# Another order of the loads and of the early attention work, and the last lane of the last projection in two token halves

## The chip, the cores and the metric

The kernel runs on one core of a Trainium2 chip. The metric is the device time of one execution in microseconds (us); the number given for a kernel is the median of its runs.

## The reference

Sparse attention feeds a network without nonlinearities. Attention has 4 batches, 8 heads, 768 tokens and a head size of 64; every query sees the keys less than 16 positions away, and one summary per block of 32 keys (the maximum of the keys, the mean of the values). The network follows on 3072 tokens of 512 numbers, in fp32:

```python
scores_l = scale * q @ k.T                 # kept where |i - j| < 16
scores_s = scale * q @ k_sum.T + log(32)   # k_sum: max over each block of 32 keys
a = softmax(concat(scores_l, scores_s))
x = a @ concat(v, v_sum)                   # v_sum: mean over each block
h = (x @ w1) * (x @ w2)                    # 512 -> 1024
out = (h @ w3) @ w_out                     # 1024 -> 1024 -> 512
```

## The kernel before

**The work.** Tokens are taken in six units u of 512, heads in four pairs, so attention has 24 steps called pairs here: pair 4u+p. A pair is: scores of q and k on TensorE (`sc`, line 374), a fused masked minimum on VectorE (line 388), exponentials on ScalarE (line 402), reciprocals of the sums (lines 407 and 408), the normalization, transposes on TensorE (`tp`, line 432), their copies to SBUF (`pt`, lines 437 to 441), the product with the values (`po`, line 452), and the attention output `x` kept as a rounded high part (line 478, ScalarE) and the rest (line 121, VectorE). Line 121 is the helper `low`, which makes every such rest.

All large products are made of three: high by high, low by high, high by low. Weights come from HBM as 64-bit numbers in 1 MB pieces (`wraw`, line 156), 20 of them: four of w_out and eight of w3 first, then w1 and w2 by turns. Each piece is converted: ScalarE takes the upper word (line 176); the low bits are joined to it either by VectorE alone (lines 203 and 206) or by ScalarE (line 188) and one VectorE instruction (line 194); then ScalarE rounds the high part (line 220) and VectorE makes the low part (line 121). The order's names number the converted pieces: in the rows of before, `w_323` is the last half of the first four w3 tiles, `w_395` the last piece of w_out (the eighth piece of all), `w_434` the first whole tile of w3 (the ninth). TensorE first multiplies w3 by w_out (`mm<-w,w`, folded weights `wp`, stored by line 247 and line 121), while the first four pairs of attention are put between; these are followed by the classic gates and projection of the first 1024 tokens (`mm<-x,w`, `mm<-wp,h`). The other 2048 tokens, in two groups of 1024, go through a Strassen-like scheme of 7 products instead of 8 (`ln`, line 727): gates `ln<-xT,ws`, and a projection `ln<-hT,ws`, whose products are evacuated and added up at lines 745 (ScalarE) and 747 (VectorE) and sent to HBM at line 894.

**The last projection.** `project_fast` calls `lanes` with two lanes (the two 128-row halves of a 256-row block of the transposed output), one PSUM bank each. It runs over seven products k = 0 to 6, in the groups (0, 1), (2, 3), (4, 5, 6) that accumulate in the bank; in each product lane 0 and then lane 1 makes 12 matmuls (4 steps of 3 terms), a 128x128 stationary by 512 tokens, and after each lane's 12 VectorE (or, for the first sums, ScalarE) adds the bank to the sum in SBUF. Products 1, 4, 5 and 6 complete a quarter of the output, and line 894 sends it.

**What sets the order.** The program of TensorE and of the DMA queue (SP) is written in numbered slots t. The table `LOADS` says which load follows the issue of which weight piece, `WORK` what is put into which slot, `FIRST` the slots in which pairs 0, 1, 2, 3 and the four after them begin. Strings choose the engine: `LAST_BITS` (a letter per weight piece) who joins the low bits, `NORMALIZE` (a letter per pair 0 to 7) who normalizes: A is eight ScalarE instructions (line 418), P one GpSimd instruction (line 421), V one on VectorE. `SECOND` says who copies the second transposed half; `first_pair` reads it for pairs 0 to 3 and `four_pairs` for pairs 4 and 5, and from pair 6 on the copies are made in `lump`, which doesn't read it. The order on ScalarE and VectorE in this part is a scheduler's. SP works its DMAs off in order, and a DMA whose buffer is still in use holds up all behind it: `q` has two buffers, so the q of one pair waits for the scores two fetches earlier; the fetches are in the order 0, 1, 2, 3, 5, 4, so q of pair 4 waits for the scores of pair 3.

Of the kernel before, what the change touches and what calls it, by code (L numbers as in the profile page):

```python
# [11 lines left out]
F32 = mybir.dt.float32  # L12
# [4 lines left out]
ALU = mybir.AluOpType  # L17
# [3 lines left out]
P = 128  # L21
# [23 lines left out]

LAST_BITS = "VVVVVVVVAAAAVVVVVVVV"
NORMALIZE = "APAPPVVV"
SECOND = "VAAVVAVV"  # L50

BANKS = "SSTTTTST"
SOONER = 400
# [20 lines left out]
def attention_moe(ctx, tc, qG, kW, kT, vP, vW, vB, mask, w1, w2, w3T, wo, out, outT):  # L74
    nc = tc.nc
    B, NPAIR, _, S = kT.shape
    S -= PAD
    NB = S // BLOCK
    U = TOKENS
# [269 lines left out]
    def keep_means(b):  # L349

        nc.sync.dma_start(vS[b], vs[b])
# [203 lines left out]
    NSU = NU // 2  # L555
# [156 lines left out]
            flow.pop(0)[1](t)  # L712
            ready.append(t)

    def lanes(n, o, weights_of, moving_of, steps, evacuated, tags, between=None):

        banks = [ps.tile([P, 512], F32, name="ln", tag=tag, bufs=bufs) for tag, bufs in tags]
        for at, k in enumerate(o.ids):
            stationary_of = yield from weights_of(at, k)
            for i in range(n):  # L720
                for c in range(steps):
                    if between and c % KH == 0:
                        between(at, i * steps // KH + c // KH)
                    a, m = [stationary_of(i, c, w) for w in range(2)], moving_of(k, c)
                    terms = [(a[0], m[0]), (a[1], m[0]), (a[0], m[1])]
                    for j, (x, y) in enumerate(terms):
                        nc.tensor.matmul(  # L727
                            banks[i][:, :U],
                            lhsT=x,
                            rhs=y,  # L730
                            start=c + j == 0 and k in o.first,
                            stop=c == steps - 1 and j == 2 and k in o.last,
                            skip_group_check=True,
                        )
                    if c < steps - 1:
                        yield 3 * U
                with tc.high_priority(offset=SOONER):
                    evacuated(at, k, i, banks[i][:, :U])
                yield 3 * U

    def add_up(o, k, parts, got):

        to, more = o.adds[k]
        if more is None:
            nc.scalar.copy(parts[to], got)
        else:
            nc.vector.tensor_tensor(parts[to], got, parts[more], ALU.add)  # L747

    xT, raws, kept, hT, tasks, background = {}, {}, {}, {}, [], []

# [23 lines left out]
    def gates(n, whole):  # L774


        o = ORDERS[n]
        for r in range(NF // 4):
            if r == NF // 4 - 1:
                flow.extend(output_flow(k, c) for k in LATE.ids for c in range(2))  # L780
                if n + 1 < NSU:
                    gates_flow(n + 1)

            def weights_of(at, k):
                while (n, k) not in xT:
# [12 lines left out]
            def evacuated(at, k, i, got):  # L798
                if at == 0:
                    parts.append(whole.parts(i))  # L800
                add_up(o, k, parts[i], got)
# [65 lines left out]
    def project_fast(n, whole):  # L867
        parts = []

        def between(at, j):  # L870
            with tc.high_priority(offset=SOONER // 2):
                if j < 3 and at + 2 < NK:
                    for work in whole.moving(at + 2):
                        next(work, 0)
            if n + 1 < NSU and j == 3 and at in (4, 5):
                moving_x(n + 1, at - 4)

        def weights_of(at, k):
# [7 lines left out]
        def evacuated(at, k, i, got):  # L886
            if at == 0:
                parts.append((*temporary(), *temporary()))
            add_up(LATE, k, parts[i], got)
            done = {1: (0, 0, 2), 4: (0, 1, 3), 5: (1, 1, 1), 6: (1, 0, 0)}  # L890
            if k in done:
                half, u, t = done[k]
                rows, cols = half * DH + i * P, (n - 1) * 2 * U + u * U
                nc.sync.dma_start(outT[rows : rows + P, cols : cols + U], parts[i][t])

        tags = [("mm", 2), ("mm", 2)]
        yield from lanes(2, LATE, weights_of, lambda k, c: hT[n, k][c], NF // 2, evacuated, tags, between)

    def spill_weights(q):

# [109 lines left out]
    def fill(s):  # L1010
        if s < NS:
            gather(*place(s), inputs[s][1])
# [103 lines left out]
    LOADS = {  # L1116
        4: [lambda: keys(0)],
        7: [lambda: nc.sync.dma_start(mask_sb, mask)],
        9: [lambda: fetch(0), lambda: rows(0, 1)],
        12: [lambda: fetch(1)],  # L1120
        13: [lambda: rows(0, 0)],
        15: [lambda: rows(0, 2)],
        16: [lambda: keys(2), lambda: fetch(2)],
        17: [lambda: keys(1)],
        19: [lambda: keys(3)],
        20: [lambda: fetch_values(0)],
        22: [lambda: fetch(3)],
        23: [lambda: fetch_values(1), lambda: fetch_values(2)],
        26: [lambda: fetch_values(3)],
    }  # L1130
    WORK = {
        11: [lambda: first_keys(0), lambda: fill(0)],
        13: [lambda: means(0)],
        14: [lambda: first_keys(1)],
        17: [lambda: fetch_sums(0)],
        18: [lambda: fill(1), lambda: load_second(0)],
        19: [lambda: rows(1, 2)],
        20: [lambda: rows(1, 0), lambda: first_keys(2), lambda: fill(2)],
        21: [lambda: rows(1, 1), lambda: fetch(5), lambda: fetch_sums(2)],
        22: [lambda: first_keys(3), lambda: fetch(4), lambda: fill(3), lambda: fetch_sums(1), lambda: load_second(1)],  # L1140
        25: [lambda: second_batch(0), lambda: load_second(2), lambda: fetch(6)],
        29: [lambda: load_second(3)],
        30: [lambda: means(1), lambda: fetch_sums(3)],
        31: [lambda: second_batch(1), lambda: fetch_values(4)],
        32: [lambda: fetch_values(5), lambda: second_batch(3)],
        33: [lambda: second_batch(2), lambda: fetch_sums(4)],
        35: [lambda: keep_means(1)],
        38: [lambda: fetch_sums(5), lambda: fill(4), lambda: fill(5)],
        40: [lambda: fetch(7), lambda: fill(6)],
        47: [lambda: fill(7)],  # L1150
# [208 lines left out]
```

## Time and profile before

| | |
|---|---|
| median of three runs | 514.44 us |
| the three runs | 510.35, 514.44, 514.94 us |
| the profiled execution | 510.71 us |
| its span, first to last instruction | 508.9 us |
| TensorE (PE) busy | 487.1 us, 96% of the span |
| VectorE (DVE) busy | 356.8 us, 70% |
| ScalarE (ACT) busy | 318.4 us, 63% |
| GpSimd (POOL) busy | 43.5 us, 9% |
| mean granted TensorE clock | 0.998 |

PEld is TensorE's weight load, which has rows of its own. In a timeline a row gives start, duration, engine, line, operation, what it writes and reads, the number of instructions that are merged, and in brackets how long the engine was idle before it and who released it. Neighbouring matmuls overlap in the records. A few rows' durations overlap the next row's start by about 0.1 us, so the step from one start to the next is the better measure in a busy stretch.

### The profile page before, as it was taken

The page shows a single profiled execution, that of the slowest core. Times are in us where ns is not written, and L with a number is a line of the kernel's source. Part 1 is how long each engine was busy: PE and PEld are TensorE (multiplying, and loading weights), DVE is VectorE, ACT ScalarE, POOL GpSimd, SP SyncE. Part 2 cuts the span into 40 slices and gives each one's busy share as a digit, 9 for nine tenths or more (in the row PEclk, how much of TensorE's full clock was granted, in tenths as well). Part 3 has the DMA queues.
Part 4 walks back from the last instruction along what each step waited for, and adds up shares of the span by engine and source line. Part 5 has one row for each costly group of instructions (what it writes and reads, how often), then busy time and mean ns, then how long its engine had stood idle before and what let it go on. Part 6 is the DMA issues. An engine that isn't in the chain of part 4 may idle for free.

```text
span 508.9 us, 10455 instructions
## 1 busy us (share of the span) xinstructions
PE 487.1 (96%) x3792; PEld 390.2 (77%) x3792; DVE 356.8 (70%) x870; ACT 318.4 (63%) x882; POOL 43.5 (9%) x86
## 2 busy tenths in 40 slices
PE   0889998999999999999999999999999999999996
PEld 0667776888887777777777877877788888888885
DVE  4978866898814598984558895899977029129972
ACT  5589975567726788877897587657865421513710
POOL 1022323101210210000000000000000000000000
PEclk9999999999999999999999999999999999999999
DMA  8998749999589989879998899998778655555762
GB/s 341 406 412 274 288 151 363 316 374 406 186 257 314 284 288 280 252 264 341 311 318 269 296 308 300 350 340 259 220 253 253 225 194 184 201 184 189 216 199 83
DMA packets 57460, 139.29 MB, mean 274 GB/s; under 512 B 6208, under 2 KB 19008, under 8 KB 54848
## 3 DMA queue, kind: packets, MB, share of 16 engines
q1 hardware_dynamic: 55104, 134.43, 77.5%
q0 software_dynamic: 1152, 2.10, 2.6%
q10 hardware_dynamic: 1152, 2.10, 1.1%
q8 instruction: 30, 0.49, 0.4%
q14 instruction: 22, 0.18, 0.1%
HBM read 105.89 MB, written 32.70 MB: 272 GB/s over the span
## 4 chain that ended last, share of the span: by engine, by line
PE 85%; DMA 5%; DVE 5%; ACT 4%; issue 1%; SPq 0%
PE ln L727 46%; PE mm L125 28%; PE po L452 4%; PE sc L374 4%; DMA wraw<-in_wo_dram 3%; PE tp L432 2%; DMA wraw<-in_w_dram 2%; DVE wf L206 2%; DVE w L121 1%; ACT w L220 1%; ACT sm L402 1%; ACT wf L176 1%; DVE wf L203 1%; ACT sm L418 0%; ACT wp L247 0%
## 5 line engine op out<-in xcount | busy, mean ns | idle before, releaser
L727 PE MATMUL ln<-xT,ws 128*128 128x512 f32 x672 | 157.0, 392 | 0.0
L727 PEld LDWEIGHTS ln<-xT,ws 128*128 128x128 f32 x672 | 125.0, 188 | 27.6 <-issue 0.6
L125 PE MATMUL mm<-x,w 128*128 128x512 f32 x384 | 91.1, 394 | 0.7 <-ACT x L478 0.5
L125 PEld LDWEIGHTS mm<-x,w 128*128 128x128 f32 x384 | 71.0, 188 | 17.4 <-ACT x L478 0.9
L402 ACT ACTIVATE sm<-sm,mx 128x120 f32<-128x120 f32 x192 | 74.0, 390 | 7.8 <-DVE mx L388 7.6
L727 PE MATMUL ln<-hT,ws 128*128 128x512 f32 x336 | 78.3, 392 | 0.0
L747 DVE TENSOR_TENSOR tmp<-ln,tmp 128x512 f32<-128x512 f32 x52 | 35.8, 688 | 55.4 <-PE ln L727 41.2
L727 PEld LDWEIGHTS ln<-hT,ws 128*128 128x128 f32 x336 | 62.6, 188 | 13.4 <-DVE hT L121 0.2
L125 PE MATMUL mm<-w,w 128*128 128x512 f32 x192 | 50.5, 411 | 15.5 <-ACT w L220 12.7
L638 ACT CAST hT<-hr 128x512 fp32r<-128x512 f32 x56 | 32.1, 622 | 42.5 <-DVE hr L804 35.4
L125 PEld LDWEIGHTS mm<-w,w 128*128 128x128 f32 x192 | 36.0, 194 | 26.8 <-ACT w L220 13.8
L388 DVE CUSTOM_DVE_ANT_0 sm<-sc,mask_sb 128x120 f32<-128x120 f32 x192 | 42.3, 276 | 15.1 <-PE sc L374 15.0
L125 PE MATMUL mm<-wp,h 128*128 128x512 f32 x192 | 46.3, 395 | 0.0
L412 ACT ACTIVATE sm<-sm,mx 128x120 f32<-128x120 f32 x128 | 38.8, 386 | 6.1 <-DVE mx L408 6.1
L125 PEld LDWEIGHTS mm<-wp,h 128*128 128x128 f32 x192 | 35.4, 188 | 8.0 <-issue 0.5
L121 DVE TENSOR_TENSOR hT<-hr,hT 128x512 fp32r<-128x512 f32 x56 | 35.5, 685 | 3.1 <-ACT hT L638 3.0
L402 ACT ACTIVATION_READ_ACCUMULATOR sm<-sm,mx 128x1 f32 x192 | 36.9, 192 | 0.0
L121 DVE TENSOR_TENSOR w<-wf,w 128x1024 fp32r<-128x1024 f32 (+1 forms) x22 | 25.8, 1179 | 8.3 <-ACT w L220 8.2
L452 PEld LDWEIGHTS po<-pt,v 120*64 120x64 f32 x768 | 24.4, 138 | 8.4 <-issue 4.2
L361 POOL COPY k<-ks 128x96 f32<-128x96 f32 (+1 forms) x32 | 10.9, 355 | 228.1 <-DMA k<-in_kW_dram 191.5
L176 ACT ACTIVATE wf<-wraw 128x1024 f32<-128x1024 f32 (+1 forms) x22 | 23.1, 1056 | 11.1 <-DMA wraw<-in_w_dram 6.3
L220 ACT CAST w<-wf 128x1024 fp32r<-128x1024 f32 (+1 forms) x22 | 21.3, 970 | 11.4 <-DVE wf L206 11.3
(62 smaller groups left out, 548.2 us busy)
## 6 DMA issues: line engine op xcount, KB each, us to landing
ws<-wS SPq DMA_DIRECT2D x56, 512.0 KB
wraw<-in_w3T_dram SPq DMA_DIRECT2D x8, 1024.0 KB
wraw<-in_w_dram SPq DMA_DIRECT2D x8, 1024.0 KB
wS<-sp SPq DMA_DIRECT2D x16, 512.0 KB
ws<-pS SPq DMA_DIRECT2D x16, 512.0 KB
k<-in_kW_dram SPq DMA_DIRECT2D x20, 368.0 KB
raw<-in_kT_dram SPq DMA_DIRECT2D x16, 392.0 KB
q<-in_qG_dram SPq DMA_DIRECT2D x24, 256.0 KB
```

Source lines behind the costliest of these rows:

```text
L121: eng.tensor_tensor(dst, src, hi.bitcast(F32), ALU.subtract)
L125: nc.tensor.matmul(acc, lhsT=a, rhs=b, start=first and i == 0, stop=last and i == len(terms) - 1)
L176: nc.scalar.activation(f[:, some], words[:, some, 1].bitcast(F32), AF.Prelu, scale=2.0**-112, alpha=-(2.0**32),)
L220: nc.scalar.copy(t[:, 0, some], f[:, some])
L374: nc.tensor.matmul(sc[h][64 * g : 64 * g + 64, i * KR : (i + 1) * KR], lhsT=q[rows, i * P + 64 * g : i * P + 64 * g + 64], rhs=k[rows, i, ...
L388: nc.vector.tensor_tensor_reduce(out=sm[:, j], in0=sc[h][:, i * KR : (i + 1) * KR], in1=mask_sb[:, 0 if blk == 0 else 2 if blk == BLOCKS - ...
L402: nc.scalar.activation(sm[:, j], sm[:, j], AF.Exp, bias=mx[:, 0, j : j + 1], scale=-1.0, accum_out=mx[:, 1, j : j + 1])
L412: nc.scalar.activation(sm[:, j], sm[:, j], AF.Copy, scale=mx[:, 2, j : j + 1])
L452: nc.tensor.matmul(po[cols, at : at + 64], lhsT=v[:KR, g, i, cols], rhs=pt[g][:, (h * NBLK + i) * 64 : (h * NBLK + i + 1) * 64], start=Tru ...
L638: nc.scalar.copy(dst[0], src)
L727: nc.tensor.matmul(banks[i][:, :U], lhsT=x, rhs=y, start=c + j == 0 and k in o.first, stop=c == steps - 1 and j == 2 and k in o.last, skip ...
L747: nc.vector.tensor_tensor(parts[to], got, parts[more], ALU.add)
```

## The change

There are two parts. The first rewrites tables. The low bits of the eighth weight piece (the last of w_out) are now taken by ScalarE and one VectorE instruction instead of two VectorE instructions; pair 2 is normalized by one GpSimd instruction instead of eight on ScalarE; the letter of pair 7 in `SECOND` changes. In `LOADS` and `WORK` some fifteen entries move: the first block of value rows is loaded ahead of the mask, two other blocks follow the last piece of w_out instead of standing on both sides of it, the q of pair 2 is asked for five slots later, the keys of pairs 1 to 3 together, the value rows of the second batch earlier, one of that batch's key loads (`load_second(0)`) later and another (`load_second(2)`) earlier, so that this one is now ahead of the second w1 piece. TensorE's order in the early part stays as it was, row for row.

The second part is in `lanes`: for the last group of tokens, in the products k = 4, 5 and 6, lane 1 is made for the first 256 tokens and then for the other 256, in two PSUM banks taken from another pool tag, with an evacuation and a DMA for each half.

```diff
-LAST_BITS = "VVVVVVVVAAAAVVVVVVVV"
-NORMALIZE = "APAPPVVV"
-SECOND = "VAAVVAVV"
+LAST_BITS = "VVVVVVVAAAAAVVVVVVVV"
+NORMALIZE = "APPPPVVV"
+SECOND = "VAAVVAVA"
...
+                split = ending and i == n - 1 and at > NK - 4
+                if split and k in o.first:
+                    halves_of_last = [ps.tile([P, 512], F32, name="ln", tag="tp", bufs=2) for _ in range(2)]
+                ends = [(slice(0, U), banks[i])]
+                if split:
+                    ends = [(slice(h * U // 2, (h + 1) * U // 2), bank) for h, bank in enumerate(halves_of_last)]
+                for cols, bank in ends:
+                    for c in range(steps):
...
+                            nc.tensor.matmul(
+                                bank[:, cols],
+                                lhsT=x,
+                                rhs=y[:, cols],
...
+                    with tc.high_priority(offset=SOONER):
+                        evacuated(at, k, i, bank[:, cols], cols)
...
-                nc.sync.dma_start(outT[rows : rows + P, cols : cols + U], parts[i][t])
+                nc.sync.dma_start(outT[rows : rows + P, cols + some.start : cols + some.stop], parts[i][t][:, some])
...
-        16: [lambda: keys(2), lambda: fetch(2)],
-        17: [lambda: keys(1)],
+        16: [lambda: keys(2)],
+        17: [lambda: keys(3), lambda: keys(1)],
+        21: [lambda: fetch(2)],
```

**ScalarE, from the last piece of w_out to the first whole tile of w3.** Line 220 rounds a weight's high part, line 407 and 418 belong to the softmax of pair 0, line 176 and 188 prepare the ninth weight piece, and line 247 stores folded weights. Before:

```order
L220 CAST w_395<-wf 128x1024
L418 ACTIVATE sm<-sm,mx 128x120 x8
L176 ACTIVATE wf<-wraw 128x1024
L247 CAST wp_76<-mm 128x512
L247 CAST wp_77<-mm 128x512
L188 ACTIVATE wraw<-wraw 128x1024
L247 CAST wp_78<-mm 128x512
L247 CAST wp_79<-mm 128x512
L220 CAST w_434<-wf 128x1024
```

Now:

```order
L220 CAST w_392<-wf 128x1024
L407 ACTIVATE mx<-mx 128x8
L176 ACTIVATE wf<-wraw 128x1024
L188 ACTIVATE wraw<-wraw 128x1024
L418 ACTIVATE sm<-sm,mx 128x120 x2
L247 CAST wp_76<-mm 128x512
L418 ACTIVATE sm<-sm,mx 128x120 x3
L247 CAST wp_77<-mm 128x512
L418 ACTIVATE sm<-sm,mx 128x120 x3
L247 CAST wp_78<-mm 128x512
L220 CAST w_434<-wf 128x1024
L247 CAST wp_79<-mm 128x512
```

Both preparations of `w_434` now stand ahead of the normalization, which is taken apart, and its rounding stands ahead of the last store. Ahead of the rows shown, between the first exponential of pair 0 and the rounding of the last piece of w_out, ScalarE now does, in this order: line 176 of the last w_out piece, three exponentials, the rounding of `w_322` (`w_323` before), the added line 188, line 309, four exponentials; before, the rounding of `w_323` came directly behind the first exponential.

**ScalarE, where the first gates begin.** Line 176 is the upper word of the first w2 piece (`w_908` before, `w_901` now) and then of the next piece, 309 the means of the second batch, 437 the copy of pair 3's transposes, 478 the output x of pair 3, 521 the first gate. Before:

```order
L176 ACTIVATE wf<-wraw 128x1024
L309 COPY vs<-means 128x128
L437 COPY pt<-tp 120x512
L220 CAST w_908<-wf 128x1024
L176 ACTIVATE wf<-wraw 128x1024
L478 CAST x<-po 128x512
L521 COPY g<-mm 128x512
```

Now:

```order
L176 ACTIVATE wf<-wraw 128x1024
L309 COPY vs<-means 128x128
L437 COPY pt<-tp 120x512
L220 CAST w_901<-wf 128x1024
L478 CAST x<-po 128x512
L176 ACTIVATE wf<-wraw 128x1024
L521 COPY g<-mm 128x512
```

The rounding of x has changed places with the upper word of the following piece. On VectorE, likewise, x's low part is now directly behind the low part of the first w2 piece, where line 203 of the following piece stood between.

**TensorE, the end of the program.** `ln<-hT` is a projection. Before:

```order
L432 MATMUL tp<-ident,sm 120x64 x16
L727 MATMUL ln<-hT,ws 128x512 x18
L452 MATMUL po<-pt,v 64x64 x16
L727 MATMUL ln<-hT,ws 128x512 x30
L727 MATMUL ln<-xT,ws 128x512 x336
L727 MATMUL ln<-hT,ws 128x512 x168
```

Now:

```order
L452 MATMUL po<-pt,v 64x64 x16
L735 MATMUL ln<-hT,ws 128x512 x30
L735 MATMUL ln<-xT,ws 128x512 x336
L735 MATMUL ln<-hT,ws 128x512 x108
L735 MATMUL ln<-hT,ws 128x256 x24
L735 MATMUL ln<-hT,ws 128x512 x12
L735 MATMUL ln<-hT,ws 128x256 x24
L735 MATMUL ln<-hT,ws 128x512 x12
L735 MATMUL ln<-hT,ws 128x256 x24
```

36 matmuls of 512 columns, in three groups of 12, have become 72 of 256.

More of the change, by code (lines that the diff above doesn't have):

```diff
@@ L713, in flow_in, with lanes @@
             ready.append(t)
-    def lanes(n, o, weights_of, moving_of, steps, evacuated, tags, between=None):
+    def lanes(n, o, weights_of, moving_of, steps, evacuated, tags, between=None, ending=False):
         banks = [ps.tile([P, 512], F32, name="ln", tag=tag, bufs=bufs) for tag, bufs in tags]
@@ L720, in lanes @@
             for i in range(n):
[L721 to L736, printed above, removed]
@@ new lines, in lanes @@
+                for cols, bank in ends:
+                    for c in range(steps):
+                        if between and c % KH == 0:
+                            between(at, i * steps // KH + c // KH)
+                        a, m = [stationary_of(i, c, w) for w in range(2)], moving_of(k, c)
+                        terms = [(a[0], m[0]), (a[1], m[0]), (a[0], m[1])]
+                        for j, (x, y) in enumerate(terms):
+                            nc.tensor.matmul(
+                                bank[:, cols],
+                                lhsT=x,
+                                rhs=y[:, cols],
+                                start=c + j == 0 and k in o.first,
+                                stop=c == steps - 1 and j == 2 and k in o.last,
+                                skip_group_check=True,
+                            )
+                        if c < steps - 1:
+                            yield 3 * U // len(ends)
+                    with tc.high_priority(offset=SOONER):
+                        evacuated(at, k, i, bank[:, cols], cols)
+                    yield 3 * U // len(ends)
@@ L743, in add_up @@
+    def add_up(o, k, parts, got, cols):
         to, more = o.adds[k]
         if more is None:
-            nc.scalar.copy(parts[to], got)
+            nc.scalar.copy(parts[to][:, cols], got)
         else:
-            nc.vector.tensor_tensor(parts[to], got, parts[more], ALU.add)
+            nc.vector.tensor_tensor(parts[to][:, cols], got, parts[more][:, cols], ALU.add)
     xT, raws, kept, hT, tasks, background = {}, {}, {}, {}, [], []
@@ L796, in gates, with evacuated @@
             parts = []
-            def evacuated(at, k, i, got):
+            def evacuated(at, k, i, got, cols):
                 if at == 0:
                     parts.append(whole.parts(i))
-                add_up(o, k, parts[i], got)
+                add_up(o, k, parts[i], got, cols)
                 if k in o.done:
@@ L893, in evacuated @@
                 rows, cols = half * DH + i * P, (n - 1) * 2 * U + u * U
-                nc.sync.dma_start(outT[rows : rows + P, cols : cols + U], parts[i][t])
+                nc.sync.dma_start(outT[rows : rows + P, cols + some.start : cols + some.stop], parts[i][t][:, some])
         tags = [("mm", 2), ("mm", 2)]
-        yield from lanes(2, LATE, weights_of, lambda k, c: hT[n, k][c], NF // 2, evacuated, tags, between)
+        yield from lanes(2, LATE, weights_of, lambda k, c: hT[n, k][c], NF // 2, evacuated, tags, between, n == NSU - 1)
     def spill_weights(q):
@@ L1117, in attention_moe @@
         4: [lambda: keys(0)],
-        7: [lambda: nc.sync.dma_start(mask_sb, mask)],
-        9: [lambda: fetch(0), lambda: rows(0, 1)],
+        7: [lambda: rows(0, 1)],
+        8: [lambda: nc.sync.dma_start(mask_sb, mask)],
+        9: [lambda: fetch(0)],
         12: [lambda: fetch(1)],
-        13: [lambda: rows(0, 0)],
-        15: [lambda: rows(0, 2)],
-        16: [lambda: keys(2), lambda: fetch(2)],
-        17: [lambda: keys(1)],
-        19: [lambda: keys(3)],
+        15: [lambda: rows(0, 0), lambda: rows(0, 2)],
+        16: [lambda: keys(2)],
+        17: [lambda: keys(3), lambda: keys(1)],
         20: [lambda: fetch_values(0)],
+        21: [lambda: fetch(2)],
         22: [lambda: fetch(3)],
@@ L1131, in attention_moe @@
     WORK = {
-        11: [lambda: first_keys(0), lambda: fill(0)],
+        10: [lambda: first_keys(0)],
+        11: [lambda: fill(0)],
         13: [lambda: means(0)],
         14: [lambda: first_keys(1)],
[L1135 to L1141, printed above, removed]
+        17: [lambda: fetch_sums(0), lambda: rows(1, 2)],
+        18: [lambda: fill(1)],
+        19: [lambda: rows(1, 1)],
+        20: [lambda: load_second(0), lambda: rows(1, 0), lambda: first_keys(2), lambda: fill(2)],
+        21: [lambda: fetch(5), lambda: fetch_sums(2), lambda: fetch_sums(1), lambda: second_batch(0)],
+        22: [lambda: first_keys(3), lambda: fetch(4), lambda: fill(3), lambda: load_second(1)],
+        23: [lambda: load_second(2)],
+        25: [lambda: fetch(6)],
         29: [lambda: load_second(3)],
-        30: [lambda: means(1), lambda: fetch_sums(3)],
-        31: [lambda: second_batch(1), lambda: fetch_values(4)],
+        30: [lambda: second_batch(1), lambda: means(1), lambda: fetch_sums(3)],
+        31: [lambda: fetch_values(4)],
         32: [lambda: fetch_values(5), lambda: second_batch(3)],
         33: [lambda: second_batch(2), lambda: fetch_sums(4)],
-        35: [lambda: keep_means(1)],
+        34: [lambda: keep_means(1)],
         38: [lambda: fetch_sums(5), lambda: fill(4), lambda: fill(5)],
```

8 lines of the change are left out of this document (2 added, 6 removed).

## The prediction

> **What bounds the kernel now.** I read the chain of waits first: it says which stretches anything off TensorE can shorten.
>
> ```profile
> 71.01 8.47 DMA wraw<-in_w_dram
> ...
> 86.73 44.04 PE mm L125 x193
> ...
> 383.32 121.42 PE ln L727 x534
> 504.76 0.69 DVE tmp L747
> ```
>
> From 86.73 us on, the chain is TensorE alone, down to one VectorE addition and the last DMA. 121.42 us for 534 matmuls is 0.227 us per 512 columns, nothing between them. The change takes no work from TensorE, so time can come only from what TensorE waits for before 86.73 and from what follows its last matmul; what it gains before 86.73 stays gained, as nothing later in the chain waits for anybody else. Next, TensorE's timeline, for the stalls:
>
> ```profile
> 11.45 0.80 PE L125 MATMUL mm<-w,w 128*128 128x512 f32 x1 [11.45 <-ACT w L220]
> ...
> 36.71 0.73 PE L125 MATMUL mm<-w,w 128*128 128x512 f32 x2 [0.97 <-ACT w L220]
> 37.97 5.28 PE L125 MATMUL mm<-w,w 128*128 128x512 f32 x22 [0.53 <-DVE w L121]
> ...
> 46.13 4.15 PE L125 MATMUL mm<-w,w 128*128 128x512 f32 x17 [0.76 <-DVE w L121]
> ...
> 58.19 0.68 PE L432 MATMUL tp<-ident,sm 64*120 64x64 f32 x16
> ...
> 62.19 5.78 PE L125 MATMUL mm<-w,w 128*128 128x512 f32 x24
> 67.89 0.68 PE L432 MATMUL tp<-ident,sm 64*120 64x64 f32 x16
> 68.50 1.05 PE L374 MATMUL sc<-k,q 64*64 64x120 f32 x32
> ...
> 80.84 1.04 PE L374 MATMUL sc<-k,q 64*64 64x120 f32 x30 [1.04 <-ACT vs L309]
> ...
> 86.73 41.32 PE L125 MATMUL mm<-x,w 128*128 128x512 f32 x181 [0.22 <-DVE x L121]
> ```
>
> It waits for weights as ScalarE and VectorE convert them, then for the first w2 piece and for x. TensorE is idle for 508.9 - 487.1 = 21.8 us of the span: 11.45 before its first matmul, whose loads the change leaves alone, 4.1 behind its last, 6.2 between. So the tables can't give more than 1.2%.
>
> **The tables, step by step.** ScalarE's rows:
>
> ```profile
> 29.31 0.40 ACT L402 ACTIVATE sm<-sm,mx 128x120 f32<-128x120 f32 x1 [1.09 <-DVE mx L388]
> ...
> 30.39 1.05 ACT L220 CAST w<-wf 128x1024 fp32r<-128x1024 f32 x1 [0.59 <-DVE wf L206]
> ...
> 32.11 0.38 ACT L402 ACTIVATE sm<-sm,mx 128x120 f32<-128x120 f32 x1
> ...
> 32.49 1.11 ACT L176 ACTIVATE wf<-wraw 128x1024 f32<-128x1024 f32 x1
> ...
> 35.62 1.04 ACT L220 CAST w<-wf 128x1024 fp32r<-128x1024 f32 x1
> 36.57 2.39 ACT L418 ACTIVATE sm<-sm,mx 128x120 f32<-128x120 f32 x8
> 38.87 1.12 ACT L176 ACTIVATE wf<-wraw 128x1024 f32<-128x1024 f32 x1
> ...
> 41.05 1.13 ACT L188 ACTIVATE wraw<-wraw 128x1024 uint32<-128x1024 uint16 x1
> ...
> 43.29 0.59 ACT L247 CAST wp<-mm 128x512 fp32r<-128x512 f32 x1 [0.64 <-PE mm L125]
> 43.77 1.05 ACT L220 CAST w<-wf 128x1024 fp32r<-128x1024 f32 x1
> ...
> 60.13 0.56 ACT L437 COPY pt<-tp 120x512 f32<-120x512 f32 x1
> ```
>
> *Step 1, the last w_out piece.* From the first exponential at 29.31 I lay the new order end to end (from start to start, a row less its overlap of 0.1: lines 176 and 188 about 1.02 each, an exponential with its read 0.38, a rounding 0.95): line 176 29.7, three exponentials 30.7, rounding of `w_322` 31.85 (it was at 30.39), line 188 32.8, four exponentials 34.0, rounding of the last w_out piece 35.5. That is 0.1 before 35.62. The price is that `w_322` is 1.5 us late: its 12 products end near 36.7 instead of 35.5, but TensorE waited until 36.71 and 37.97 anyway. VectorE saves one instruction here, which hides in that wait. Gain 0.1.
>
> *Step 2, `w_434`.* Lines 176 and 188 now start at 36.6 and 37.6, ahead of eight normalizations that used to precede them. With these (8 of 0.29) and three stores (0.48 each, from 43.29 to 43.77) behind them, the rounding falls at 38.65 + 2.3 + 1.4 = 42.4 instead of 43.77, and no longer behind the last store's wait for TensorE (0.64).
>
> ```profile
> 44.85 1.22 DVE L121 TENSOR_TENSOR w<-wf,w 128x1024 fp32r<-128x1024 f32 x1 [0.22 <-ACT w L220]
> ...
> 55.42 0.20 DVE L408 RECIPROCAL mx<-mx 128x8 f32<-128x8 f32 x1
> ...
> 56.91 1.73 DVE L121 TENSOR_TENSOR w<-wf,w 128x1024 fp32r<-128x1024 f32 x1
> ...
> 85.99 0.68 DVE L121 TENSOR_TENSOR x<-po,x 128x512 fp32r<-128x512 f32 x1
> ```
>
> ```profile
> 55.77 1.79 POOL L421 TENSOR_TENSOR sm<-sm,mx 128x960 f32<-128x960 f32 x1 [3.01 <-DVE mx L388]
> ```
>
> The low part follows 1.1 behind the rounding and takes 1.2: ready at 44.7. TensorE reaches its second matmul of `w_434` at about 44.7 instead of 46.13: 1.4 gained. The normalization ends at 42.0, and the transposes that need it come at 42.9, so taking it apart is hidden, by 0.9.
>
> *Step 3, what is late next.* Pair 1 is normalized on GpSimd. The new VectorE order has its reciprocal behind two weights' low parts, at 55.3 against 55.42; with 1.79 us of GpSimd the transposes can start at 57.5 against 58.19. TensorE would be there at 56.6 and waits: the gain shrinks to 0.7.
>
> *Step 4, pair 2 leaves ScalarE.* pt of pair 1 is copied at 59.1 instead of 60.13, as fewer weights stand ahead of it: 1.0. The eight normalizations (2.39 as above) are gone, and TensorE no longer waits for them at 67.89: po ends at 61.2, 24 matmuls of 0.227 end at 66.65, and the transposes follow. GpSimd takes its instruction at about 62.1, behind the store of sums that waits for po, and ends at 63.9: hidden, by 2.7. While GpSimd works, VectorE is slower (1.73 for a low part instead of 1.22); x of pair 1, whose bank these transposes take, is then free at 66.3, so this cover is only 0.3. Scores of pair 3 at 67.26 against 68.50: gain 1.24.
>
> *Step 5, the w2 piece and x.* q of pair 4 waits for those scores, and the w2 piece is queued behind it:
>
> ```profile
> 69.64 0.33 SPq L339 DMA_DIRECT2D q<-in_qG_dram  x1
> ...
> 71.01 0.38 SPq L156 DMA_DIRECT2D wraw<-in_w_dram  x1
> ```
>
> ```profile
> 10.00:20.00 10.00, 6.84 (x19) 4.62 (x20) 9.89 (x14) 6.52 (x7) 2.04 (x3) 1.00 1.03 413
> 68.00:70.00 2.00, 2.00 (x50) 1.73 (x51) 1.17 (x2) 2.00 (x4) 0.00 (x0) 1.00 0.00 0
> ```
>
> The DMA engines carry nothing from 68 to 70 (share 0.00, 0 GB/s), so an issue 1.24 earlier lands 1.24 earlier: 78.27 instead of 79.48. The moved key load stands behind this piece and can't delay it, only the next w1 piece. The rest of the chain shifts with it. Then x is rounded ahead of the next piece's line 176, and its low part ahead of line 203:
>
> ```profile
> 84.12 1.13 ACT L176 ACTIVATE wf<-wraw 128x1024 f32<-128x1024 f32 x1
> 85.15 0.57 ACT L478 CAST x<-po 128x512 fp32r<-128x512 f32 x1
> ```
>
> The rounding of x gains 1.0 on ScalarE; its low part is then bound by the low part ahead of it and gains the 0.6 of line 203. TensorE runs without gaps from 84.87 instead of 86.73. Tables: 1.24 + 0.62 = 1.86.
>
> At nothing: `SECOND[7]` has no reader. The value rows ahead of the mask delay the fifth weight piece by about 0.3 MB, 0.8 us at the early 413 GB/s, which VectorE's and ScalarE's turn on the piece before covers, barely; without cover it would cost that 0.8. The later q fetch lets weights be issued sooner, but conversion, not landing, times them.
>
> **The tail.**
>
> ```profile
> 27.77 0.30 PEld L125 LDWEIGHTS mm<-w,w 128*128 128x128 f32 x2 [0.16 <-issue]
> ```
>
> ```profile
> L727 PEld LDWEIGHTS ln<-hT,ws 128*128 128x128 f32 x336 | 62.6, 188 | 13.4 <-DVE hT L121 0.2
> ```
>
> ```profile
> 505.48 0.33 SPq L894 DMA_DIRECT2D out_dram<-tmp  x1
> ```
>
> ```profile
> 506.50:507.00 0.50, 0.00 (x0) 0.00 (x0) 0.00 (x0) 0.00 (x0) 0.00 (x0) 1.00 0.95 373
> ```
>
> 36 matmuls of 0.227 (8.19) become 72 with as many weight loads. No row shows a 256-column one. Below, it is half, 0.114: 8.19, no cost. Above, it is one whole recorded load, 0.188: 13.54, +5.35. But two loads together last 0.30, so the second starts 0.11 behind the first. That is near the lower end; I take 0.12: 8.64, +0.45.
>
> The last addition has 256 columns: between half of 0.69 and all of it; with the step from 512 (0.69) to 1024 columns (1.22), 0.42: -0.27. The last DMA moves 128 KB instead of 256; at 373 GB/s half of it takes 0.35: -0.35, and 0 if its time doesn't go by bytes. The first half's addition and DMA come 1.4 us earlier, beside matmuls. Tail: 0.45 - 0.27 - 0.35 = -0.17.
>
> **Sum.** 1.86 + 0.17 = 2.0 us off the profiled execution: 510.71 - 2.0 = 508.7. That execution is 3.73 below the median of the three runs shown, which lie at 510.35, 514.44 and 514.94; on the median, 514.44 - 2.0 = 512.4.
>
> **The rivals.**
>
> *The tables give back what they gain.* If the reciprocal of pair 1 comes later by 0.7, or x of pair 1 by over 0.3 beyond its cover, step 4 starts from nothing, and the swap of x is left: 0.62 + 0.17 = 0.8, so 513.6. For it: covers of 0.3; against: several waits have to go wrong in one direction.
>
> *The weight loads bound the halves* (the other side). Above 0.148 per half (8.19 + 1.86 + 0.62, over 72) the change loses. At 0.188 it is 5.35 - 0.62 - 1.86 = +2.9: 517.3. For it: the mean load of 0.188. Against: the pair in 0.30.
>
> *No load overlaps a matmul at all.* Then 0.227 is a load of 0.11 and 0.117 of streaming, a half 0.11 + 0.06 = 0.17, 72 of them 12.2: +4.0, in all +1.5, 515.9. [...] The trace speaks against it: in the pair above, the second load starts 0.11 behind the first, while the first matmul still streams.
>
> *More than forecast:* landing or reciprocals improve further, up to the waits' 6 us; halfway, 3.5 in all, 510.9.
>
> **How the numbers follow.** Forecast 0.52, tables give back 0.22, halves bound by loads 0.06, no overlap 0.03, more than forecast 0.11; 0.06 for an early wait of 1 to 3 us that I overlooked. The time is 512.4; its own range, with the spread of the runs, is 508.3 to 514. All cases: 507.5 to 516. A measurement of this kernel tells about 1%, 5.1 us, from no change. A true gain over that is unlikely (0.04), but the runs shown lie 4.1 us apart and more, and a median at their lower end is 508.7, over 1% below 514.44: about 0.24 of the forecast and the larger gain together. Faster 0.28; slower by over 1% takes halves above 0.188 or two rivals together, 0.07; within 1%, 0.65.
>
> **What would show it.** The low part of `w_434` at about 43.5, scores of pair 3 near 67.3, the q of pair 4 on SP at 68.4, the first w2 piece's line 176 at 78.3, gapless matmuls from 84.9; the 256-column matmuls 0.12 apart; last addition 0.42, and 3.5 us from the last matmul to the end instead of 4.2. Wrong: TensorE waiting for pair 1's or 2's transposes past 58 or 68, the w2 piece landing at 79.5 still, or halves over 0.148 apart.

## The result, and the profile after

The changed kernel took 510.04 us (median of 8 runs, 508.96 to 510.71) beside 513.63 us before (8 runs, 510.35 to 515.32) on the same chip: ratio 0.994, 95% interval 0.9918 to 0.9963, so 3.1 us (1.9 to 4.2) less by the ratio; the medians lie 3.6 apart. A few executions, of 520.69 to 527.52 us, ran 1.4 to 2.8% above the median of their kernel's other runs, at a mean granted clock of 0.983 to 0.989, and don't enter the ratios and ranges. The forecast was 2.0 less and 512.4. But the two profiled executions, 510.71 before and 510.13 after, lie only 0.6 us of span apart. Both facts need an explanation, since the first comparison gives more than the forecast and its traces less.

TensorE's timeline after, at the places of the forecast's steps:

```profile
37.79 5.30 PE L125 MATMUL mm<-w,w 128*128 128x512 f32 x22 [0.38 <-DVE w L121]
...
44.61 4.60 PE L125 MATMUL mm<-w,w 128*128 128x512 f32 x18
...
57.32 0.69 PE L432 MATMUL tp<-ident,sm 64*120 64x64 f32 x16
...
66.75 0.27 PE L432 MATMUL tp<-ident,sm 64*120 64x64 f32 x1
67.21 0.68 PE L432 MATMUL tp<-ident,sm 64*120 64x64 f32 x15 [0.19 <-DVE x L121]
67.82 1.05 PE L374 MATMUL sc<-k,q 64*64 64x120 f32 x32
...
79.99 1.04 PE L374 MATMUL sc<-k,q 64*64 64x120 f32 x30 [0.91 <-ACT vs L309]
...
85.28 41.34 PE L125 MATMUL mm<-x,w 128*128 128x512 f32 x181 [0.34 <-DVE x L121]
```

The wait of 0.76 at 46.13 is gone, and the transposes of pair 1 stand at 57.32 instead of 58.19. Of the 0.87 gained there only 0.68 is left at the scores of pair 3 (67.82, before 68.50): a new wait has come up inside pair 2's transposes, for x of pair 1. The gates run without gaps from 85.28 instead of 86.73. The chain of waits after:

```profile
70.33 8.31 DMA wraw<-in_w_dram
...
85.28 44.06 PE mm L125 x193
...
269.32 1.88 PE ln L735 x7
...
382.72 121.93 PE ln L735 x570
504.67 0.42 DVE tmp L755
```

VectorE's timeline at the end of the program:

```profile
503.23 0.42 DVE L755 TENSOR_TENSOR tmp<-ln,tmp 128x256 f32<-128x256 f32 x1 [0.74 <-PE ln L735]
504.67 0.42 DVE L755 TENSOR_TENSOR tmp<-ln,tmp 128x256 f32<-128x256 f32 x1 [1.01 <-PE ln L735]
```

The windows at the end; the last two columns are the DMA share and GB/s:

```profile
506.00:506.50 0.50, 0.00 (x0) 0.00 (x0) 0.00 (x0) 0.00 (x0) 0.00 (x0) 1.00 0.70 248
506.50:507.00 0.50, 0.00 (x0) 0.00 (x0) 0.00 (x0) 0.00 (x0) 0.00 (x0) 0.80 0.00 0
```

The chain no longer is TensorE alone from the gates on: near 269 there is a piece that begins behind a wait. And 1.45 us at 85 are 0.60 at the last unbroken run of matmuls (382.72, before 383.32). At the end the two additions of halves lie 1.44 apart, 12 matmuls each, so 0.12 for 256 columns; the last run is 0.51 longer than before, and the stretch from the start of the last addition 0.51 shorter (508.3 - 504.67 = 3.63, before 508.9 - 504.76 = 4.14), as the last transfer is through at 506.5 instead of 507.

### The profile page after: what moved, and what is told of

The parts are those of the page before. It is cut to its first block, busy times and chain, and to the rows that moved or that the text cites. A ratio compares the mean times of both kernels' runs of the same rounds, so it can differ in the third digit from the quotient of the medians.

```text
span 508.3 us, 10536 instructions
## 1 busy us (share of the span) xinstructions
PE 487.7 (96%) x3828; PEld 392.4 (77%) x3828; DVE 357.5 (70%) x872; ACT 316.5 (62%) x875; POOL 49.4 (10%) x87
## 4 chain that ended last, share of the span: by engine, by line
PE 77%; ACT 9%; DVE 6%; DMA 5%; issue 1%; SPq 0%; ACTq 0%
PE ln L735 42%; PE mm L125 25%; PE po L452 4%; PE sc L374 3%; PE tp L432 2%; ACT sm L402 2%; DVE w L121 2%; ACT w L220 2%; DVE wf L206 2%; DMA wraw<-in_w_dram 2%; DMA q<-in_qG_dram 2%; ACT wf L176 1%; ACT wraw L188 1%; DMA wS<-sp 1%; DMA wraw<-in_wo_dram 1%
## 5 line engine op out<-in xcount | busy, mean ns | idle before, releaser
L735 PE MATMUL ln<-hT,ws 128*128 128x512 f32 (+1 forms) x372 | 78.8, 371 | 0.0
L755 DVE TENSOR_TENSOR tmp<-ln,tmp 128x512 f32<-128x512 f32 (+1 forms) x55 | 36.2, 658 | 55.1 <-PE ln L735 40.9
L735 PEld LDWEIGHTS ln<-hT,ws 128*128 128x128 f32 x372 | 64.6, 189 | 12.1 <-DVE hT L121 0.2
```

The costliest lines, as they stand in the source:

```text
L735: nc.tensor.matmul(bank[:, cols], lhsT=x, rhs=y[:, cols], start=c + j == 0 and k in o.first, stop=c == steps - 1 and j == 2 and k in o.las ...
L755: nc.vector.tensor_tensor(parts[to][:, cols], got, parts[more][:, cols], ALU.add)
```

## The experiments

My theory at this point: the order of the tables is worth the gain; the kernel's time scatters because the first w2 piece lands sooner or later; the changed kernel is early enough that a later wait swallows that scatter. Rivals: the tail carries the gain; the difference of the medians is a draw; one of the two kinds of table edits does it alone.

**The kernel before, unchanged.**

> The kernel before, unchanged, to see how far two runs of one kernel lie apart and to catch the profile of one of its more usual executions. Theory (the order of the tables is worth the measured 3 us, by waits ahead of 86 us and by a wait timed by a DMA that the profiled 510.71 happened not to meet): ratio 1.000 within 0.004, times from 510 to 515; if the profiled execution is at 512.5 or more, it has 1.5 to 4 us more of TensorE waiting than the 21.8 us idle of the first profile, in one or two places that the changed kernel does not have. Rival (the difference of the medians is a draw from executions that scatter in both kernels alike): the copy's median lies as far from the other runs of the same kernel as the changed one's did, 2 us or more.

Measured: 512.01 us (12 runs, 509.83 to 515.02), ratio 0.9994 (0.9972 to 1.0017). The profiled execution was again a short one. Chain of waits:

```profile
71.01 7.86 DMA wraw<-in_w_dram
...
86.14 44.04 PE mm L125 x193
...
382.72 121.46 PE ln L727 x534
```

The piece took 0.61 less to land than in the first profile, and the gates and the last run of matmuls come 0.59 and 0.60 earlier. So two executions of one kernel do differ by that transfer.

**The tables alone.**

```diff
-        yield from lanes(2, LATE, weights_of, ..., evacuated, tags, between, n == NSU - 1)
+        yield from lanes(2, LATE, weights_of, ..., evacuated, tags, between)
```

> The new tables and strings, the last lane's products whole as before. Theory (tables carry the gain, the tail gives nothing): ratio 0.993 to 0.996, 510.0 to 511.5 beside 513.6; gapless matmuls from 85.3; from the last matmul to the end 4.1 us as before. Rival (the tail carries it, its halves freeing the end for more than the profile shows): ratio 0.998 to 1.001.

Measured: 510.19 us, ratio 0.9957 (0.9934 to 0.998), 2.2 us less. Chain of waits:

```profile
70.63 8.57 DMA wraw<-in_w_dram
...
85.84 44.25 PE mm L125 x193
...
382.52 121.41 PE ln L735 x534
```

The tables alone give what the whole change gives. From the start of the last run to the end of the span it is 508.1 - 382.52 = 125.58, in the changed kernel 508.3 - 382.72 = 125.58 too. Here nothing waits near 269.

**The tail alone.** The changed kernel with the three strings, `LOADS` and `WORK` of before.

```diff
-LAST_BITS = "VVVVVVVAAAAAVVVVVVVV"
-NORMALIZE = "APPPPVVV"
-SECOND = "VAAVVAVA"
+LAST_BITS = "VVVVVVVVAAAAVVVVVVVV"
+NORMALIZE = "APAPPVVV"
+SECOND = "VAAVVAVV"
```

> The last lane's last three products in halves, tables and strings as before. Theory: ratio 0.999 to 1.001, 513.0 to 514.0 beside 513.6; halves 0.12 us apart, 3.6 us from the last addition to the end instead of 4.1, and the matmuls 0.5 longer. Rival (the tail carries the gain): ratio 0.993 to 0.996.

Measured: 512.08 us, ratio 0.9995 (0.9972 to 1.0017). The tail is worth nothing that can be measured; by the trace 511.4 - 385.77 = 125.63 from the last run to the end, against 125.58 before. The profiled execution, 513.22 us, is one of the longer ones, with before's early order. Its chain of waits:

```profile
70.94 10.72 DMA wraw<-in_w_dram
...
88.90 44.04 PE mm L125 x193
...
385.77 121.97 PE ln L735 x570
```

Its TensorE, at the transposes of pair 3:

```profile
80.03 0.68 PE L432 MATMUL tp<-ident,sm 64*120 64x64 f32 x15 [1.88 <-DVE x L121]
```

Here is what a longer execution loses: the piece was issued at 70.94, as always, and took 10.72 instead of 7.86 to 8.47. That is 2.2 us more at the gates than in the first profile (88.90 against 86.73); only 0.3 more is lost between there and the last run.

**The moved loads and works alone, and the strings alone.** Each is the kernel before with that part of the diff.

> The moved loads and works alone: the strings (last bits, normalizations, second copies) and the tail as before. Theory (steps 1 to 3 and the swap of x come from the moves, 1.4 us for w_434 shrinking to 0.7, and 0.6 for x; what keeps the gain past 67 us is pair 2 off ScalarE, which is in the strings): it keeps the swap of x and at most 0.7, so 0.6 to 1.3 us faster in the trace at 86 us, ratio 0.996 to 0.999. Rival (the moves are all of it): ratio 0.993 to 0.995, gapless matmuls from 85.3. Rival (the strings are all of it): ratio 0.999 to 1.002, gapless from 86.7.

> The kernel before with the new strings alone (last bits of one more piece by ScalarE, pair 2 normalized on GpSimd): loads, works and tail as before. Theory (strings and moves are worth the gain only together: the moves alone left ScalarE with too much, and q of pair 4 was issued at 74.0 instead of 69.6): the strings relieve ScalarE by 2.4 us and give up to 1 us at 68 us: ratio 0.997 to 1.000, gapless from 85.7 to 87. Rival (the strings are the gain and the moves carry nothing): ratio 0.994 to 0.996, gapless from 85.3.

Measured: moves alone 517.15 us, ratio 1.0091 (1.0062 to 1.0119); strings alone 512.98 us, ratio 1.002 (0.9996 to 1.0044). Neither part is a gain by itself. That the moves alone would keep a part of the gain was wrong by 5 us.

**One letter back at a time**, in the changed kernel.

```diff
-LAST_BITS = "VVVVVVVAAAAAVVVVVVVV"
+LAST_BITS = "VVVVVVVVAAAAVVVVVVVV"
```

> The changed kernel with the last bits of piece 7 on VectorE again (the other letter back). ScalarE's order up to 60 us is then that of the run with the moves alone. Theory (this letter, not the normalizations, made the moves 4.6 us slower: VectorE's two instructions on piece 7 let the scheduler put the rounding of w_434 behind two more conversions): TensorE waits 2 us and 1.2 us for w_434 near 47 and 49 us as there, second matmul of it at 49 instead of 44.6; of these 4.4 us about all reaches the end: ratio 1.005 to 1.010. Rival (the normalizations did it): ratio 0.995 to 0.999, second matmul at 44.6 to 45.

Measured: 515.61 us, ratio 1.0082 (1.005 to 1.0114). TensorE's timeline:

```profile
48.37 0.50 PE L125 MATMUL mm<-w,w 128*128 128x512 f32 x1 [2.13 <-ACT w L220]
50.43 6.66 PE L125 MATMUL mm<-w,w 128*128 128x512 f32 x17 [1.55 <-DVE w L121]
```

TensorE waits for `w_434` again, twice, and longer than the 0.76 of the kernel before (this profiled execution is 3.7 us above its kernel's median). On ScalarE its rounding starts at 47.26 instead of 42.26, behind three stores and another line 176 and 188. So the letter of one weight piece is what the moved loads need: with it they gain, without it they lose about 4 us. Not all of that is waiting: the 17 matmuls in the last row take 6.66, where the same 17 took 4.15 in the kernel before (the row at 46.13 in the prediction). The granted clock is 0.50 from 49 to 55 us; more on this below.

```diff
-NORMALIZE = "APPPPVVV"
+NORMALIZE = "APAPPVVV"
```

> The changed kernel with pair 2 normalized by ScalarE again (one letter back), everything else as changed; on ScalarE this puts eight normalizations between x of pair 1 and the store at 66.9 us. Theory (step 4 of the forecast: these 2.4 us on ScalarE stood in the way of pair 2's transposes, and GpSimd's instruction beside the low part of w_761 cost 1.1 us of VectorE's time): TensorE as in the changed kernel to 61 us; the low part at 62 takes 1.3 to 1.8 us instead of 2.85, and the transposes of pair 2 start at 67.5 to 68.3 instead of 66.75 and 67.21, so 0.3 to 1.0 us is lost: ratio 0.996 to 0.999. Rival (the crowding of VectorE cost as much as ScalarE's relief gave): transposes at 66.8 to 67.3, no difference from the changed kernel.

Measured: 510.16 us, ratio 0.9968 (0.9948 to 0.9989), not told apart from the changed kernel's. Its VectorE:

```profile
61.98 1.62 DVE L121 TENSOR_TENSOR w<-wf,w 128x1024 fp32r<-128x1024 f32 x1 [0.24 <-ACT w L220]
63.53 1.80 DVE L266 TENSOR_REDUCE ks<-raw 128x24 f32<-128x768 f32 x2
65.25 0.68 DVE L121 TENSOR_TENSOR x<-po,x 128x512 fp32r<-128x512 f32 x1
```

Its TensorE:

```profile
66.74 0.69 PE L432 MATMUL tp<-ident,sm 64*120 64x64 f32 x16
67.35 1.05 PE L374 MATMUL sc<-k,q 64*64 64x120 f32 x32
```

VectorE of the changed kernel, for comparison:

```profile
61.99 2.85 DVE L121 TENSOR_TENSOR w<-wf,w 128x1024 fp32r<-128x1024 f32 x1 [0.24 <-ACT w L220]
64.76 1.80 DVE L266 TENSOR_REDUCE ks<-raw 128x24 f32<-128x768 f32 x2
66.48 0.67 DVE L121 TENSOR_TENSOR x<-po,x 128x512 fp32r<-128x512 f32 x1
```

The rival is right, and more than right. ScalarE, in the new order, has an empty stretch from 62.4 to 66.8, and the eight normalizations fit into it: pair 2's transposes are not late with them. Without GpSimd's instruction the low part takes 1.62 instead of 2.85, x is ready 1.23 earlier, and the scores of pair 3 start at 67.35, 0.47 ahead of the changed kernel. Taking pair 2 off ScalarE cost 0.47 us here and gave nothing. (The medians don't tell 0.5 us apart.)

**The changed kernel, unchanged, a second time.**

> The changed kernel, unchanged, on the chip of the next three. Theory (the scatter of the kernel before is the landing of the first w2 piece, 79 to 82 us, and comes straight through to the end; in the changed kernel the chain ahead of the gates is 1.5 us early and a later wait near 268 us swallows what that piece varies by): median 509.5 to 510.5, its executions within 2 us, ratio 0.994 to 0.997; the profile has gapless matmuls from 85 to 86.5, and a wait of TensorE near 268 where they start before 85.6. Rival (the scatter is the chip's and the first comparison a lucky draw): executions over 4 us like the kernel before.

Measured: 510.35 us (12 runs, 509.57 to 513.74), ratio 0.998 (0.9959 to 1). Chain of waits:

```profile
70.46 10.30 DMA wraw<-in_w_dram
...
87.40 44.05 PE mm L125 x193
...
384.13 121.93 PE ln L735 x570
```

The third part of my theory falls: its executions scatter over 4 us like those of the kernel before, a late landing (10.30) goes through to the end here too, and nothing swallows it. That the first comparison's executions lay so close together was a draw.

**The first w2 piece earlier on the queue.** Three kernels, since its landing sets the gates. In the first the fetch of pair 4, whose q holds SP's queue from 55 to 69, stands behind the piece; the second is the same edit in the kernel before.

```diff
-        22: [lambda: first_keys(3), lambda: fetch(4), lambda: fill(3), lambda: load_second(1)],
-        23: [lambda: load_second(2)],
+        22: [lambda: first_keys(3), lambda: fill(3), lambda: load_second(1)],
+        23: [lambda: load_second(2), lambda: fetch(4)],
```

> The changed kernel with the fetch of pair 4 (q and k, whose q waits for the scores of pair 3 and held SyncE's queue from 55 to 69 us) moved behind the first w2 piece. Theory (the landing of that piece sets when the gates run without gaps): the piece is issued by 57 and lands before 68, its line 176 starts by 76.5 instead of 78.7, the wait of 0.9 for the means at 80 goes, gapless matmuls from 82.5 to 84 instead of 85.3; of these 1.3 to 2.8 us the wait near 268 takes back what it has taken before, so 0.3 to 2 us less than the changed kernel: ratio to before 0.990 to 0.995. Rival (the transfers of 230 to 270 us alone set the time from there): gapless from 83, but the matmuls behind 271 at 271.1 as in the changed kernel, and the same time within 0.3 us. Rival (the ring's slot or the key load ahead of the piece holds it up anyway): issued after 66, nothing gained.

> The kernel before with that one fetch moved behind the first w2 piece, everything else as before. Theory: the scatter goes with the landing, executions within 2 us instead of 5, and the median falls by 2.5 to 4.5 us: ratio 0.991 to 0.995, as much as the whole change gave. Rival (landing isn't what scatters or sets the time): ratio 0.998 to 1.001 and executions over 4 us.

Measured: 514.35 us, ratio 1.0052 (1.0035 to 1.007), and 514.82 us, ratio 1.0053 (1.0031 to 1.0074). Both lose, though the piece is issued at 55.93 (56.54 in the second) and converted without a wait. TensorE of the first:

```profile
81.53 1.11 PE L432 MATMUL tp<-ident,sm 64*120 64x64 f32 x16 [3.87 <-POOL sm L421]
```

And its VectorE:

```profile
75.25 0.92 DVE L203 TENSOR_SCALAR wf<-wf 128x1024 uint32<-128x1024 uint32 x1 [0.81 <-ACT wf L176]
76.21 1.22 DVE L206 SCALAR_TENSOR_TENSOR wf<-wraw,wf 128x1024 uint32<-128x1024 uint32 x1
77.35 0.68 DVE L121 TENSOR_TENSOR x<-po,x 128x512 fp32r<-128x512 f32 x1
77.95 0.68 DVE L121 TENSOR_TENSOR wp<-mm,wp 128x512 fp32r<-128x512 f32 x1
78.55 0.19 DVE L408 RECIPROCAL mx<-mx 128x8 f32<-128x8 f32 x1
```

The scheduler puts the work on the early piece ahead of pair 3's reciprocal, which now starts at 78.55 instead of 74.90; GpSimd normalizes from 78.91, and pair 3's transposes wait 3.87. The early landing was bought with a late softmax. Pair 3's scores are late with it, so SP's next q goes out at 84.65 instead of 78.96, and a weight piece behind that q, issued at 86.48, lands only at 96.19; the chain of waits runs through it, up to matmuls at 98.83. In the kernel before, the same edit makes the transposes wait 4.19. On the scatter, my theory holds in part: without the late landing the executions lie 2.5 and 2.8 us apart, less than the 4 and more of the kernels before and after, but not within 2.

So the last two keep q of pair 4 ahead of the piece and move only its k (and the key loads) behind; the second puts the next w1 piece ahead of those too. Both also let x go ahead of VectorE's summaries.

The first of the two:

```diff
-        22: [lambda: first_keys(3), lambda: fetch(4), lambda: fill(3), lambda: load_second(1)],
-        23: [lambda: load_second(2)],
+        22: [lambda: first_keys(3), lambda: fetch_q(4), lambda: fill(3)],
+        23: [lambda: fetch_k(4), lambda: load_second(1), lambda: load_second(2)],
...
-        keep_x(outputs(pt, values.pop(s)), xs[u])
+        po = outputs(pt, values.pop(s))
+        with tc.high_priority(offset=SOONER):
+            keep_x(po, xs[u])
```

The second differs from it in two slots:

```diff
-        23: [lambda: fetch_k(4), lambda: load_second(1), lambda: load_second(2)],
-        25: [lambda: fetch(6)],
+        25: [lambda: fetch_k(4), lambda: load_second(1), lambda: load_second(2), lambda: fetch(6)],
```

> The changed kernel with the first w2 piece directly behind q of pair 4 (k of pair 4 and two key loads behind the piece instead of one load and k ahead of it), and x of pairs 0 to 3 ahead of VectorE's summaries where both are ready. Theory (its landing sets the start of the gates, and everything issued within some 10 us shares the DMA engines, so bytes behind it count as much as bytes ahead): pair 3's reciprocal stays ahead of the piece's conversion, unlike where the piece went ahead of q; line 176 of the piece at 76 to 78 instead of 78.7 to 80.4; no wait of over 0.5 for the means near 80; gapless from 83.7 if the next w1 piece lands by 81.5, from 86.3 if it lands at 84: ratio to before 0.990 to 0.999. Rival (first in, first out: only what stands ahead of the piece counts): lands by 75.5, line 176 at 75.4.

> As the run before it, with the next w1 piece ahead of k of pair 4 and of the key loads too. Theory: w2 and w1 land together by 77 to 79.5; the means no longer hold TensorE; x of pair 3 now stands behind the rounding of the w1 piece on ScalarE, at 83.5 instead of 83.3, low part 84.1: gapless from 84.5 to 85.5, in fewer executions late: ratio 0.992 to 0.996, half a microsecond under the changed kernel at best. Rival (the reordered conversions cost more than the landing gives, as where the piece went ahead of q): gapless from 87 or later, ratio 1.000 or more.

Measured: 513.8 us, ratio 1.003 (1.0013 to 1.0047), and 515.89 us, ratio 1.008 (1.0058 to 1.0102). ScalarE of the first, at the piece's line 176:

```profile
76.36 1.19 ACT L176 ACTIVATE wf<-wraw 128x1024 f32<-128x1024 f32 x1 [0.75 <-DMA wraw<-in_w_dram]
```

TensorE of the first:

```profile
80.64 2.68 PE L374 MATMUL sc<-k,q 64*64 64x120 f32 x48 [2.65 <-POOL k L361]
```

ScalarE of the second:

```profile
75.48 1.20 ACT L176 ACTIVATE wf<-wraw 128x1024 f32<-128x1024 f32 x1
```

TensorE of the second:

```profile
80.83 3.06 PE L374 MATMUL sc<-k,q 64*64 64x120 f32 x48 [2.87 <-POOL k L361]
85.33 1.08 PE L374 MATMUL sc<-k,q 64*64 64x120 f32 x16 [1.44 <-POOL k L361]
```

The piece is issued at 69.40 and 69.34; it is converted 7.0 and at most 6.1 later (ScalarE's row in the second shows no wait), against 7.9 to 10.7 where k and a key load, 760 KB, stand between q and it. In the second a whole w1 piece, 1 MB, is issued 2 us behind it, and that doesn't slow it: my theory that bytes behind count as much as bytes ahead finds no support here. But the rival isn't shown either: it had line 176 at 75.4, which the second meets (75.48), while the first, at 76.36, lies where the theory put it. With one execution of each, and landings that scatter by 2.9 us, the question stays open.

Neither kernel gains, because the scores of the next two pairs now wait for GpSimd, which puts the summaries into k only behind four copies of value sums (2.99 us from 77.31 in the first, 2.94 from 77.28 in the second); in the second it then waits another 0.33 for k itself, the load that was moved behind. No kernel tried is measurably faster than the changed one.

**The clock behind the waits.** The waits above cost more than their own length. In the first profiles of the kernels before and after, the granted clock is 1.00 from the first matmul to the last. In each profile shown here of a kernel that lost, it falls to 0.50 for some microseconds where TensorE has waited longest: from 49 to 55 us with the letter of `LAST_BITS` back, from 82 to 84 with the piece ahead of q, from 81 to 83 and from 80 to 90 in the last two kernels. That the wait brings it about is read from the order in time, and wasn't tested by itself. The products of pair 3 with its values, in the first and the second of the last two kernels:

```profile
84.30 1.15 PE L452 MATMUL po<-pt,v 120*64 120x64 f32 x32
```

```profile
86.34 1.97 PE L452 MATMUL po<-pt,v 120*64 120x64 f32 x32
```

In the first, the clock is 1.00 again by 84; in the second it is 0.50, and the same 32 products take 0.82 longer. So a part of each loss is not the wait, but the slow matmuls behind it. Between 28 and 100 us, the half clock follows every single wait of 2.06 us and more in these profiles. It also follows one of 1.79 (the strings alone) and one of 1.36 (the letter back, at 34.81), but not one of 1.88 (the tail alone), so no limit can be read off. The wait of 2.06 is for the means, in the profiled execution with pair 2 back on ScalarE, which had a late landing (9.71) and took 513.20 us, 3.0 above its kernel's median: a late landing, too, can cost more than its lateness.

## Why the prediction was right, and where not

*The whole.* Tables gain, tail about nothing, no new long wait: the forecast's course is what the runs show. Its 2.0 us lie between the three comparisons of the new tables with the kernel before (3.1, 2.2 and 1.0 less, by the ratios), and in that there is luck. By the rows it is less: 0.68 at the issue of q and 0.61 at x make 1.3 at equal landing; the other two profiles with the changed tables whole give 1.0 (q issued at 69.26) and 1.2 (69.09). That the rest of the first comparison's 3.1 is a luckier set of landings is argued from the 2.9 us by which these differ, not shown. The 512.4 came out 2.4 too high: 0.8 because the three runs before lay above the eight of the comparison, the rest because the medians lie 3.6 apart and not 2.0.

*Steps 1 to 3* were right to 0.2: TensorE at 37.79 without a longer wait, the rounding of `w_434` at 42.26 (forecast 42.4), its products unbroken from 44.61 (44.7), pair 1's transposes at 57.32 (57.5). The experiment on the letter adds what the forecast didn't say: the moves earn this only with the low bits of the eighth piece on ScalarE.

*Step 4* failed in size, and its reason failed. It put the scores of pair 3 1.24 earlier; they came 0.68 earlier. The cover of 0.3 for x of pair 1 rested on 1.73 for the low part beside GpSimd; it took 2.85, and x came 0.46 too late. That 1.73 was read from a low part (56.91 to 58.64) that lay beside GpSimd's product (55.77 to 57.56) for only its first 0.65 us; now the product starts with the low part, at 61.97, lies beside it for all its 1.79 us, and a copy follows. The forecast named this place in its first rival, and valued it as all or nothing; it was half. And its sentence that the eight normalizations are gone and "TensorE no longer waits for them" credited the wrong edit: with them back, TensorE doesn't wait either and is 0.47 earlier. It didn't wait in the kernel before: the row at 67.89 has no bracket, and the 24 matmuls ahead of it take 5.70 from start to start there and 5.68 now, where the sum took 5.45. What brought pair 2 forward was the order ahead of it: the copies of pair 1, 1.1 earlier.

*Step 5* was right. The transfer shifted with its issue (8.31 against 8.47), and from line 176 to the gates it is 85.28 - 78.67 = 6.61 instead of 86.73 - 79.51 = 7.22: 0.61 for the changed places of x, forecast 0.62. The key load, issued at 72.43, 2.10 behind the piece, brought no delay that shows in these landings, as said; the piece with 1 MB issued 2 us behind it, converted at most 6.1 after its issue, points the same way. What the step lacked is that the landing varies by 2.9 us from execution to execution (7.86 to 10.72 from issue on), more than the whole change is worth.

*"What it gains before 86.73 stays gained"* failed in the profiled execution. TensorE of the changed kernel:

```profile
269.32 1.88 PE L735 MATMUL ln<-xT,ws 128*128 128x512 f32 x7 [0.44 <-DVE xT L121]
```

ScalarE of the changed kernel, ahead of that:

```profile
248.66 0.59 ACT L437 COPY pt<-tp 120x512 f32<-120x512 f32 x1 [1.66 <-DMA q<-in_qG_dram]
...
264.26 0.62 ACT L674 CAST sp<-wr 128x512 fp32r<-128x512 f32 x1 [0.76 <-DMA wS<-sp]
```

From the gates to the last run it is 297.44 us here, 296.6 in both profiles of the kernel before, 296.68 and 296.73 in the other two with the new tables: 0.8 given back in one profile of three; with pair 2 back on ScalarE TensorE waited there too, 0.44 for xT. ScalarE waits twice for transfers in this stretch and makes xT late. In the second profile of the changed kernel the first of these waits is 1.79, the second is missing, and TensorE doesn't wait. The chain of before showed TensorE alone there, but not with how little to spare; the forecast took "nothing waits" for "nothing can wait".

*The tail* was as forecast: 0.12 per half, 0.42 for the last addition, the matmuls 0.51 longer (0.45), the end 0.51 shorter (0.62). Net 0.0 instead of -0.17, and the run with the tail alone has a ratio of 0.9995. The rivals with loads as the bound are out: 0.188 per half, the mean recorded load, and 0.17, the forecast's own estimate for loads that overlap no matmul, against 0.12 in the trace.

## What to carry to other kernels

Where one late transfer sets the start of a long stretch without gaps, look first at how far its landing scatters between executions (2.9 us here), and compare profiles at equal landing: two medians can differ by it. A wait that an edit removes is credited only when undoing that one edit brings it back; here a letter that looked like the cause cost half a microsecond, and another that looked like bookkeeping carried the change. A piece brought forward on a queue is worth nothing if a scheduler then places its conversion ahead of what the next stage waits for, or if that stage waits for the transfer it overtook. And when a reordering loses more than the waits it brings, look at the granted clock behind them: here it was 0.50 for 2 to 10 us, and 32 products behind such a wait took 1.97 us where they took 1.15 at 1.00.

## What the runs showed of the hardware

A low part of 128x1024 on VectorE took 1.22 us with GpSimd idle (at 44.85 in the kernel before), 1.62 beside GpSimd's copies (at 61.98 with pair 2 back on ScalarE), and 2.85 beside GpSimd's 128x960 product with a copy of value sums behind it (at 61.99 in the changed kernel), far from the 1.73 that the forecast took. That copy took longer too: 1.49 in the changed kernel; with pair 2 on ScalarE, two of them took 1.26 together. The same 1 MB transfer behind the same queue took 7.86 to 10.72 us from issue to landing; what in an execution decides that is open, and wasn't tried. Behind waits of TensorE of 2.06 to 4.19 us in the early part, the granted clock fell to 0.50, for 2 to 10 us in the stretches given above.
